# A new hand-written order of all steps in a gated-recurrence kernel followed by an MLP

## The chip, the core and the metric

The kernel runs on one core of a Trainium2 chip. The metric is device time in microseconds (us) of one launch. It is measured over several launches, and a separate launch is profiled; the profile is one execution and has its own time.

## What is computed

The first half is a gated linear recurrence with a complex decay, for 4 batches, 8 heads, 768 tokens and 48 features a head. Its output, 3072 tokens of 384 features, goes through an MLP with 2048 hidden features and a leaky activation with one slope a feature.

```python
scale = np.minimum(mag, 0.999) / (mag + 1e-06)          # mag = |a|
a_re_n, a_im_n = (a_re * scale, a_im * scale)
for t in range(S):
    new_re = ar * S_re - ai * S_im
    new_im = ar * S_im + ai * S_re
    S_re, S_im = (new_re + kv, new_im)                  # kv = outer(k_t, v_t)
    y[:, :, t] = einsum('bhd,bhde->bhe', q[:, :, t], S_re)

h = x @ w_in                                            # x: (3072, 384)
g = np.maximum(h, 0.0) + alpha * np.minimum(h, 0.0)
out = g @ w_out
```

All of it is float32; the MLP's weights arrive as float64 words and are turned into float32 on the core.

## The kernel before

The 768 tokens of a batch are cut into 6 chunks of 128; 4 batches give 24 **units**. The decays are prepared for whole chunks at a time by nine **gate tasks** (one chunk, then two, then seven times three). A gate task is a long alternation of DVE and ACT operations (lines 248 to 427, some small ones on POOL). It writes its decays to DRAM (line 321) and, at its end, its phases (the products of lines 422 and 425 on DVE, then the transfers of line 427).

A unit loads its queries and keys (KQ, lines 575 and 577), its phases (PP, line 586), its decays (T, line 593) and its values (V and VL, lines 602 to 628). It then runs:

- the rotation of KQ by PP, one DVE operation of 2.3 us (line 648);
- six levels of doubling block size. A level copies weights on ACT (W, line 719), makes 16 products of 32x32 on PE (line 662), multiplies KQ by decays on DVE (line 701) and masks the products into A (line 686 on DVE, 683 on ACT);
- 8 transposes on PE (line 736), copied to KT by ACT (line 738), and the outer products of keys and values (line 747), which DVE adds into the state St (lines 777 and 780);
- the unit's output in PSUM: 4 products that clear it (line 759), 48 products A x VL (line 768) and 16 **state products**, the earlier state times the queries (line 793);
- ACT's copy to yT (line 807) and two stores to DRAM (line 812).

The MLP runs over 14 groups of tokens: two of one unit, ten of two, two of one. A group loads x (xT, line 825), makes 16 hidden blocks of 3 products each (`features`, line 841; 256 tokens wide, 128 in the groups of one unit), applies the activation on ACT and DVE (lines 848 and 850), and adds 16 output products of 384 columns for each 128 tokens (`outputs`, line 860). Rows then leave through ACT (line 870) and line 873.

Everything that sets who comes first is **one string, ORDER**. Each task is a Python generator that stops at every step; a letter resumes the task of that letter. A to I are the gate tasks, J the loads of KQ, PP and T, K the transfers that spread the values' rows, L the loads of V and VL, M the raw weights, N and O their conversion, P to Z and a to m the 24 units, n the loads of x, and o the whole MLP. The instructions reach each engine's queue in the order in which the letters emit them, and an engine works its queue in that order. All DMAs are issued by SP, so a letter also fixes a transfer's place on SP's queue. Buffers (three of KQ, one of PP, two of T, one of V and VL, two of xT, two PSUM tiles for hidden blocks) bound how far a task can run ahead. The arguments of the `yield`s, such as `PE(0.47, ...)`, are costs for the planner that made ORDER; at run time `step` returns None and nothing is read from them.

```python
    def run(self, order):
        for c in order:
            next(self.tasks[self.LETTERS.index(c)], None)
```

```python
    with tc.manual_schedule():
        for i, g in enumerate(GATES):
            plan.add(gates(i, *g))
        ...
        plan.add(loads_x())
        plan.add(all_mlp())
        plan.run(ORDER)
```

Of the kernel before, what the change touches and what calls it, by code (L numbers as in the profile page):

```python
# [27 lines left out]


ORDER = (  # L30
    "AAAAAAAAAABBAMMABMAAAAAMNAAAMMAAAAAAAAABKAAAAAAJKBBNBAKJANAAAJONNAAAAAAOBNOAAAAAAAAAAAJAAAKKAAAAAAKK"
# [9 lines left out]
    "LLLLLLooooUTooULLooEooooULJETDTooDooooooDDTDUoooTTooooLooDUoDooKLTTDooooTToooooDDDTETToUUoooTooToTTT"
    "TTnoDoooooooooTLLLUUoooKooLLLLLUTUoLooLooFEJLTUUUULoooooEoJUEooooooUUUUUUEJooEULEEooooooooUoTKEEEToo"
    "EEUVoTToTUUoEoooVVoooooEooooooVUJVVoUFoVUUooTVoUVVUVEUUJJJJUEEEEEEEEEEEEUoUJJTLTVUVFVoVoFWooFVJVVooo"
    "VFooooUUUVVVJUWVKVVUVWWoooooVLLWLLLLLWLLEEEEEEEEEEEEEEEELVVoVLLoWWoLJVVoWoVUoVWVVVooEooooJEEUWWWoVVV"
    "VWVVVVoWWJJJJJJXooEFnFooEEoEELLLLLLLLKJEFLoooVEoooEEooLEooWLLLWXoWLooooWWEoooEooooKEXEWWWKoVVooooooo"
    "KXooEooooXWJWJXXoooWooooWWFoVVoWVXWooooooWWFXFWWWFEWWFFFFGFXooLJLLLLLLXWooooooWFWFXXJFoooFooooFWoFXX"
    "oLLFoGooooJJooooooJFoWFXXXFWFFFWFFFoFooWFoXFFWXooooooFooooooooooXXXXYooooooooGJFWWFXXFXYooFFoooXLLXX"
    "LFFooooooooooLoooYXGLoooXJoooooGYXXFXXFFXXXXXFFFFFFFJYYFJnYJXoGYoooooJFFFFFFFFFFFFFFFLFJJYZFoooooooL"
    "ooGoYZYXXXGJYYZooXooZZoGoooooYooYXoFooooYYYYYYYYYZZoooZFZFFFooooFXJYZoLLLoYoYJYoLLLLLLLKYoYoYooZGLLY"
    "YKYYYYJFYZYYJKXFFFGGooYYJYLLLJLFFLoooooaFFFoYLFFFoFoJJJooZLFZYYYGYYaGLoLLoLLooooooooFLLFoFFFoooooooo"  # L50
    "ooooZoooaZaJZaoooGoZaJZnGZZZZZaooooooooooooaaooaGaZZoooaooZoJoooJGoZZooZoZoooZaHZZZGGoGGGGGGGZZZZZGZ"
    "GaZKKHLGGGoooooaGGoooooooGooobooGoaoooaoaaaaaoooLoGGbooobbZaaaoaaZooaJZZZLJoLLLLLLLLLLoGGGGaaoooGboG"
    "GJoooZaJJoabboooooooaaaaaaaaGHJZHGJJbbbbGGGLGGooooooHoooobaobJJaGGGGGGGGaaaooJJboocooooooobbcoGGbcHb"
    "ooGbLJJKooooooooooooocbGbHcHcLGLcGGKooooooLLbHbLcbbaabGGGGGGooooobbKcGbGJGJGcLLGGGooooHGGcobbbcHoooo"
    "bbLooooLLLLbbbnbcGHbbbbbJGGGdoooooGoLLoocbGGGGGccbooooJJboooGKobGGoGHooLLLLLLoooGHbbbboLooooooooGcLL"
    "LdddccccHdooooocccooooooocdcccdooJoddoLoooooHJcdocLHdJoHdHKHdcoJJooooooocccccIIccoccceooJJooHLLLoooo"
    "oooLoLdeLcHHcccHHHHccccoLLLHHLHHHHnooHoHHHLooooooooHJooooeIdLLLooooooooddooooooeeeHHHHdooHoHHdHeeooo"
    "oooooodddddeooooooodJdoJoeooHHHHHHHHHHHoodoodododeoododooodeedddddddHHdHHHHHHIeeKKeeKHJJooJfooooIooo"
    "ooeeeKeddfoLLdeeooeoeoooJooLooooddLLHHHHHHHHHHHHHHJeedIeeeLfooLLoLLooefLLLLeIofdooeeeHHeeeeeeHHefIIf"
    "IfHfJHHJHJdJooooooeeJJJJJeeeoeegLJHLHHLLofoLLLLLLLofIoooooooooIHooLJffooJoHoooooHogofHoHHIoooooIoooo"  # L60
    "noffoHHooooogfoofoooooffIffffLgoogoooofgooLoffIfJoofoIfIIooJoIfoofooooffffffffffgKggooooohLLLooLhogo"
    "oIoLgghgoooooJJILLLoooLLLffILLfhIIIgghoooooooooohgooJJhgfJJfhhKffggIgggKgooohoooohhggggJghooohoogogo"
    "IgIgooooggIgggggggIhJhoLLgLgIIIIJgIogooooKKoIoooIhooLooILhIoooooooggKJIIIIIIIIJJoooooiLIhoooIIIIoIoo"
    "oooihnooIhhhhihhiooooIiooooLLLLLLiihhLLohohoooooohohohoooohhIIIIhhIhhhhhhJJJIooooooooooJJLiioihiioio"
    "JIoLooLiiijoooooIIIooooIIIioIIIIIIIIIIoiiiiiihhhhhjLLhjLoLLLLLLLiJIIIIIIIoooooojooooojoiijjjoooiooio"
    "jiiooooiLhIIIIIoIoioiiiiiiJLLLLLILooooooLLoooiIioooiiiiiIijjoIiiiIIooooooooooooonJooJJJJooojjjjooooo"
    "ooooooooooooJoLLjjoojojjoojoLkojLjjoooooooooojjkokoooooojjkkjookkoooojjjooLooooLjkjjjjJkkooojjkjjkoo"
    "oooJoooooooookJJokjjJJLllLooLokLkoLoLLLjjkkLkkkLLLLLkkjJjjkooooooooooooJkollkokkJoooooooooookllllooj"
    "kokooJJJlJokoooookkkkJkkkkkkkkkllLLlkLLooomkkkoooolooooooLollooooolloJooomloooonoooooooooooooooooooo"
    "oooooooooollllJlmmooooooooooolmmlooooooolllooolLLLLolomLLLLLllooooooooollloolmlmmmmoooooooomlllloooo"  # L70
# [882 lines left out]
```

## Time and profile before

| what | us |
|---|---|
| median of 3 runs | 863.18 |
| lowest and highest of them | 861.69, 864.44 |
| time of the profiled execution | 859.8 |
| span of its instructions | 858.1 |
| PE busy (matmuls) | 704.7 |
| DVE busy | 655.6 |
| ACT busy | 427.1 |
| POOL busy | 186.3 |
| hidden products (line 841), busy | 303.4 |
| output products (line 860), busy | 297.5 |
| decay products on KQ (line 701), busy | 178.3 |

The span runs from the first instruction to the last; the profiled execution's own time has 1.7 us more. Busy times of different engines overlap, so they don't add up to the span: an engine matters in the stretch where the others wait for it. PE busy counts matmuls as they overlap in its pipeline, and a busy PE may be slow, because its granted clock was below full in parts of the first 275 us. A matmul of two float32 operands appears as two records, as does its weight load; so counts on PE are twice the products in the code, except for the transposes and for line 759.

The first hidden product of the third group (the first group of two units) starts at 246.82 us; the last rows leave after the last output product, at the end of the span.

### The profile page before, as it was taken

Reading aid. Unit: us, or ns where it says so; the run is one execution under the profiler, and the core shown is the slowest. Engines: PE = TensorE matmul, PEld = TensorE weight load, DVE = VectorE, ACT = ScalarE, POOL = GpSimd, SP = SyncE. Lnnn points to the kernel's source line nnn. Section 1 sums busy time; section 2 is a strip of 40 time slices with the busy share of each in tenths; the row PEclk is TensorE's granted clock in tenths of the full one; section 3 lists DMA queues with packets and bytes.
Section 4 is the critical chain, followed back from the end, with each engine's and each line's share of the span. In section 5 each row is a group of like instructions: output and inputs, shape, how many; then the busy total and the mean of one; then the engine's idle time right before and its main releaser. Section 6 shows DMA issues by size and latency. Waiting matters only on the chain.

```text
span 858.1 us, 26855 instructions
## 1 busy us (share of the span) xinstructions
PE 704.7 (82%) x11488; PEld 529.1 (62%) x11488; DVE 655.6 (76%) x996; ACT 427.1 (50%) x913; POOL 186.3 (22%) x293
## 2 busy tenths in 40 slices
PE   0000414976898999999999999999999999999998
PEld 0000313655676777777777777777777777777776
DVE  5999999999976899789978987798867665444212
ACT  7757578576434565554555554654334234233221
POOL 5212323457313200440034005300052000000000
PEclk9999965896999999999999999999999999999999
DMA  7689977977688778669684787865674766221110
GB/s 222 170 211 232 269 175 178 241 154 154 170 194 165 159 195 207 125 135 227 160 182 110 180 216 147 158 170 127 176 155 74 173 121 134 63 51 38 39 39 9
DMA packets 194559, 130.92 MB, mean 153 GB/s; under 512 B 74504, under 2 KB 186248, under 8 KB 194440
## 3 DMA queue, kind: packets, MB, share of 16 engines
q1 hardware_dynamic: 194440, 129.20, 64.9%
q8 instruction: 90, 1.47, 0.8%
q14 instruction: 29, 0.24, 0.1%
HBM read 100.82 MB, written 35.71 MB: 159 GB/s over the span
## 4 chain that ended last, share of the span: by engine, by line
PE 74%; DVE 15%; SPq 3%; issue 3%; DMA 3%; ACT 2%; DVEq 0%; ACTq 0%
PE ps_o L860 29%; PE ps_h L841 29%; PE ps_lv L662 5%; PE ps_y L768 4%; DVE KQ L701 3%; PE ps_kv L747 3%; PE ps_y L793 3%; SPq L556 2%; DVE gate L336 2%; PE ps_kt L736 2%; DMA V<-in_v_dram 1%; DVE gate L338 1%; DVE gate L316 1%; DVE gate L296 1%; DVE gate L422 1%
## 5 line engine op out<-in xcount | busy, mean ns | idle before, releaser
L841 PE MATMUL ps_h<-xT,w_in_sb 128*128 128x256 f32 (+1 forms) x1344 | 303.4, 357 | 0.0
L860 PE MATMUL ps_o<-w_out_sb,g_sb 128*128 128x384 f32 x768 | 297.5, 501 | 7.2 <-DVE g_sb L850 7.1
L841 PEld LDWEIGHTS ps_h<-xT,w_in_sb 128*128 128x128 f32 x1344 | 233.8, 193 | 69.9 <-issue 1.7
L701 DVE TENSOR_TENSOR KQ<-KQ,T 96x1024 f32<-96x1024 f32 x144 | 178.3, 1248 | 44.1 <-PE ps_lv L662 41.1
L848 ACT ACTIVATE g_sb<-ps_h 128x256 f32<-128x256 f32 (+1 forms) x224 | 78.9, 353 | 235.8 <-PE ps_h L841 235.1
L850 DVE SCALAR_TENSOR_TENSOR g_sb<-g_sb,al,ps_h 128x256 f32<-128x256 f32 (+1 forms) x224 | 97.5, 437 | 126.8 <-ACT g_sb L848 126.4
L860 PEld LDWEIGHTS ps_o<-w_out_sb,g_sb 128*128 128x128 f32 x768 | 137.4, 192 | 58.0 <-DVE g_sb L850 9.7
L662 PE MATMUL ps_lv<-KQ,W 96*32 96x32 f32 x3840 | 56.5, 205 | 57.5 <-ACT W L719 54.1
L719 ACT COPY W<-KQ 96x512 f32<-96x512 f32 x120 | 74.3, 623 | 55.4 <-DVE KQ L701 54.1
L662 PEld LDWEIGHTS ps_lv<-KQ,W 96*32 96x32 f32 x3840 | 44.6, 116 | 83.0 <-ACT W L719 62.4
L662 PE MATMUL ps_lv<-KQ 96*32 96x32 f32 x768 | 12.0, 206 | 68.2 <-DVE KQ L648 52.6
L511 POOL TENSOR_SCALAR top<-top 128x768 f32<-128x768 f32 x16 | 43.5, 2721 | 84.3 <-ACT top L503 84.0
L648 DVE TENSOR_TENSOR KQ<-KQ,PP 96x2048 f32<-96x2048 f32 x24 | 55.0, 2292 | 0.0
L662 PEld LDWEIGHTS ps_lv<-KQ 96*32 96x32 f32 x768 | 9.5, 119 | 71.8 <-DVE KQ L648 52.6
L336 DVE TENSOR_TENSOR gate<-gate 128x576 f32<-128x576 f32 (+5 forms) x84 | 48.3, 575 | 3.1 <-ACT gate L308 1.3
L768 PE MATMUL ps_y<-A,VL 64*48 64x64 f32 x2304 | 42.2, 223 | 8.6 <-issue 6.8
L683 ACT ACTIVATE A<-ps_lv,rows 128x64 f32<-128x64 f32 x144 | 39.2, 331 | 19.4 <-PE ps_lv L662 19.0
L336 POOL TENSOR_TENSOR gate<-gate 128x72 f32<-128x72 f32 x42 | 19.0, 451 | 127.2 <-ACT gate L366 124.4
L768 PEld LDWEIGHTS ps_y<-A,VL 64*48 64x48 f32 x2304 | 39.6, 125 | 11.0 <-issue 8.9
L422 DVE TENSOR_TENSOR gate<-gate 128x1152 f32<-128x1152 f32 (+2 forms) x36 | 43.5, 1233 | 0.1
L807 ACT COPY yT<-ps_y 48x256 f32<-48x256 f32 x96 | 32.0, 366 | 21.1 <-PE ps_y L793 20.4
L686 DVE TENSOR_TENSOR A<-ps_lv,mask 128x256 f32<-128x256 f32 x96 | 39.5, 414 | 0.0
(100 smaller groups left out, 774.5 us busy)
## 6 DMA issues: line engine op xcount, KB each, us to landing
T<-decs SPq DMA_DIRECT2D x48, 384.0 KB
PP<-phs SPq DMA_DIRECT2D x48, 193.5 KB
KQ<-in_q_dram SPq DMA_DIRECT2D x48, 192.0 KB
decs<-gate SPq DMA_DIRECT2D x7, 1152.0 KB
...
```

The source lines that it names most:

```text
L336: on(4 * k).tensor_tensor(out=m, in0=w[:, 1::-1].unsqueeze(2).to_broadcast([P, 2, 2, k]), in1=pairs_of(u), op=ALU.mult)
L422: TT(out=m[:, a], in0=U5[:, 1 + a], in1=turned(off3, o)[:, a].unsqueeze(1).unsqueeze(3).to_broadcast([P, L // 2, nb, 2]), op=ALU.mult)
L511: nc.gpsimd.tensor_scalar(out=top, in0=top, scalar1=F64_SMALL, scalar2=None, op0=ALU.max)
L648: nc.vector.tensor_tensor(out=KQ, in0=KQ, in1=bass.AP(tensor=PP.tensor, offset=PP.offset, ap=[PP.ap[0], (1, 2), (P + 1, H), (1, P)]), op=A ...
L662: nc.tensor.matmul(t[64 * i + j:64 * i + j + HC // 2, p], lhsT=weights(4 * i + p)[:, j:j + HC // 2], rhs=q_[:, m * g:m * (g + 1)], start=T ...
L701: nc.vector.tensor_tensor(out=x, in0=x, in1=m, op=ALU.mult)
L719: nc.scalar.copy(W.rearrange("p n t -> p (n t)").rearrange("p (m h) -> p m h", h=h), halves(KQ[:, 1].rearrange("p n t -> p (n t)"), h)[:, ...
L768: nc.tensor.matmul(o, lhsT=Vp[h][64 * i:64 * i + 64, s, e_ * D:(e_ + 1) * D], rhs=a, start=False, stop=False)
L841: nc.tensor.matmul(p, lhsT=w_in_sb[:, f // 2, kk, f % 2 * P:(f % 2 + 1) * P], rhs=x_of[m][:, kk], start=(kk == 0), stop=(kk == NK - 1))
L848: nc.scalar.activation(gt, p, AF.Relu, scale=-1.0)
L850: nc.vector.scalar_tensor_tensor(out=gt, in0=gt, scalar=al_1[:, f:f + 1], in1=p, op0=ALU.mult, op1=ALU.add)
L860: nc.tensor.matmul(sums[0], lhsT=gt[:, c * P:(c + 1) * P], rhs=w_out_sb[:, f], start=(f == 0), stop=(f == NF - 1))
```

## The change

Only ORDER changes. The new string has the same 4316 letters, each as often as before, so the same instructions with the same operands are made. The first 10 letters and the last stretch of o's stay; between them nearly every stretch differs. Instructions of one task keep their order among themselves; what moves is how the tasks interleave on PE, DVE, ACT, POOL and SP.

```diff
 ORDER = (
-    "AAAAAAAAAABBAMMABMAAAAAMNAAAMMAAAAAAAAABKAAAAAAJKBBNBAKJANAAAJONNAAAAAAOBNOAAAAAAAAAAAJAAAKKAAAAAAKK"
-    "KBABKLMAMKKKAAAAAAAAAAAAABBAAAAAAAAAALLLNLNOBBBBBBBBBBBBBBBOKKLJBBJBCOCNBBBBNNBBBNNNKNBBNNBBBBBOPBBO"
-    "BBOOBBBBBBBLLBBBBBPCPPBBBBBBBBBBBOBJBBBBCBBBNBCBBJBPMMJBLBBBLBOPBLMLJJJPPBBCLBOBONOPBBMCCCCCPNPPCLCN"
...
-    "NQRoRQKoQQQRDKDJQEREoDONJDDDMDDDQooooDoDooooooRQooooooQooEDoooDoRRRRoooOooOOooooooDRRRJRoJDSooooooRD"
-    "RoRRLooQQooELoSOOOLLLLLLLDDDLLLRQQQSRRKKoLDEooSoQooOoDRooRooLoSoDoooEDDooRoooRRROSRRRREoooooQRREDDDD"
...
+    "AAAAAAAAAAAABBMJJBAAAAAAABJJBAAAMMAAAAAAAMNNMBBNLAAAAAAAAAAMNAAAAAAAAONAAAAAALLLLLLLAAAAAABOBAANAAABA"
+    "ABMLLAABBBBAAOAABBABANKKKLAKKKBKKKKKKKKMLNAKAONBOKAAAMANAABOBBBAABABAAABABAABBBBBBBOBKBBNOBBBBBBBNBB"
+    "BBBBJJNONBBBNOBNBOBOBBBJJBBPOPBBBBBBBBNCBPCPBOBBBBMKBBBBPOBOMJCPBOBBBJJOBBBNBCCKPNCCCCBBBJMLPPBNONNP"
...
+    "RCQNOnLCCLOMLCCQCCCLQLLLQOOKCOQoONNCNCooDJKKCCCRCooCoCLQDQQJDLQoQDDRDDRoQoDDoDooooooooDDNLDKRRRooQoo"
+    "QoQDDooQooooJQNJEREoooDKQoDQMDQDQDLDDDQoLLLLLLLLLoooooDDSDQEoRRODRDoooEoooooDREQQNooSDQRooooDoRDRRRD"
...
```

More of the change, by code (lines that the diff above doesn't have):

```diff
@@ L30 @@
 ORDER = (
-    "AAAAAAAAAABBAMMABMAAAAAMNAAAMMAAAAAAAAABKAAAAAAJKBBNBAKJANAAAJONNAAAAAAOBNOAAAAAAAAAAAJAAAKKAAAAAAKK"
-    "KBABKLMAMKKKAAAAAAAAAAAAABBAAAAAAAAAALLLNLNOBBBBBBBBBBBBBBBOKKLJBBJBCOCNBBBBNNBBBNNNKNBBNNBBBBBOPBBO"
-    "BBOOBBBBBBBLLBBBBBPCPPBBBBBBBBBBBOBJBBBBCBBBNBCBBJBPMMJBLBBBLBOPBLMLJJJPPBBCLBOBONOPBBMCCCCCPNPPCLCN"
-    "CCCNNCCOPPKJCPCCJMPPJJJJPCNCOCCCCCCCCPOOOOCCCONNNPPQQCOCMCMDPPPPPPPPPPPPPPPPPNPPCNCNCCCNCPONPOCCCQCN"
-    "NPKCQCCCPCPCJQQQPQQQCCCCOCCCCQCPNOJQQCOJDJPJJPPKQPDDONJDQCCCCCCCCCQCCOOCQCDQQOLOCCCCCCCDKMRnQQQMKQQK"
@@ L36 @@
-    "KKNCKOKOCCCCKMRJQoOCCQQQQNQoJCDQoCCOCLOCCNCCQONLoooLLLDLLDNNDLLDoooDDLoRoNLoRDoRNNDRDRooLLNRJRRDDDDD"
-    "NQRoRQKoQQQRDKDJQEREoDONJDDDMDDDQooooDoDooooooRQooooooQooEDoooDoRRRRoooOooOOooooooDRRRJRoJDSooooooRD"
-    "RoRRLooQQooELoSOOOLLLLLLLDDDLLLRQQQSRRKKoLDEooSoQooOoDRooRooLoSoDoooEDDooRoooRRROSRRRREoooooQRREDDDD"
-    "SDDDDDDoDEESJJSJEEQDJJRJJJSKSSSTSDDLLLRRRRRRLLLESSSDLLTSDEnToTDDSTSETTSSSSLSJTSSSLLDDDDDDDDEEDDDDooS"
-    "LLLoKTSooJSoEooSEoDDDDSEETSSSSSSJJSSSSETTTDJEEETDJooEEEEoUTJJJJLLoEooEEJTooDSoooooEoooTDDDTDoSSSSSoL"
@@ L41 @@
[L41 to L70, printed above, removed]
@@ L71 @@
-    "ooooooooooomlmlmlmoolommllllnoooooooooooooommLmmmoooooooooooooooooooooooooomoLomLooooomommoLLLLLoooL"
-    "LLmmmLLooooooooooooooooooooooooooooooooooooooooooommmmmmmmmoommmmmoooooomnoooooooooooooooooooooooooo"
+    "AAAAAAAAAAAABBMJJBAAAAAABJJBAAAMMAAAAAAAMNNMBBNLAAAAAAAAAAMNAAAAAAAAONAAAAAALLLLLLLAAAAAABOBAANAAABA"
+    "ABMLLAABBBBAAOAABBABANKKKLAKKKBKKKKKKKKMLNAKAONBOKAAAMANAABOBBBAABABAAABABAABBBBBBBOBKBBNOBBBBBBBNBB"
+    "BBBBJJNONBBBNOBNBOBOBBBJJBBPOPBBBBBBBBNCBPCPBOBBBBMKBBBBPOBOMJCPBOBBBJJOBBBNBCCKPNCCCCBBBJMLPPBNONNP"
@@ new lines @@
+    "CBBPCCOOCCNPOCCCPCPPPMCCCCLJJJDCPCPMPCNNNKCJPDNQCOCPCNCMCOPPPPCCQJPPPJJPJJJPPPPCCCCQCCQQQCDPPCCNOOCK"
+    "OPPNCCCQCNNONCPQCQPQPCCPCCCPCPMDLPCOCQCPOCCCPRJOPCNPCJCCCQQPPCCNCOCCLLPQMJCQCCDCQROQQCCCKJNLCCRCKRNR"
+    "RCQNOnLCCLOMLCCQCCCLQLLLQOOKCOQoONNCNCooDJKKCCCRCooCoCLQDQQJDLQoQDDRDDRoQoDDoDooooooooDDNLDKRRRooQoo"
+    "QoQDDooQooooJQNJEREoooDKQoDQMDQDQDLDDDQoLLLLLLLLLoooooDDSDQEoRRODRDoooEoooooDREQQNooSDQRooooDoRDRRRD"
+    "ooRRQQRoQQoooDooRDDDooRRRRRRDNNNDDOJLooJLDDDDDDSSQLoooDoLQoRRRRSRRORRESRRROSoooooSSoJJoNoooSSKSEDDJJ"
@@ new lines @@
+    "JJJJJDLoTEJSDDDSSEERDooODSSoEODRETDJTOTSEoDDTTSSSSSOSLTTLRoJnLooRKOTESSLLLLTSJooEToSLSLSDLLoooLooLDD"
+    "DDDDDDDDDDDSJEDDEKTKKEKSKoooDooooDDoSREoRESSSSSESToSLLSULDEooSTSoooooDoooDLLTTEoToooooEooEDTJTSELLLS"
+    "LLEELLSUESDDLJoLDTTSDDoooToooooDTSTooTooooooDoTooooJJooTTooUUoTToooooJTDJUooTUTTonEETTTTDEoDToDDoooo"
+    "ooUoooooLLooUEooooooooTUETEoooEoUTUooLLLLLLooEooooELLoLUJEFoooooooEEULooooTUEEEEEEEoUoooUooooUUUTToJ"
+    "UoLUooTVooVEEEUUUUUooVUooToooUoJVUEEJEEEEEJoJUoVVoVUUJoVoUUUUUUEVVUFVoTVJJEEEEEEEJJVVoooVVVVVWoooooF"
@@ new lines @@
+    "ooEJVLLEVVVKFTLLEVUEEEEEVoUWWoWEEEVooooWoEEUUVVUoVEVWWWFooooVVooooVLLLUFLVLLLLLooLJVWWoUUWoooEEEEooV"
+    "VJWWVVVEWJoVJJEVFJoLnVFEVVEWJoVVEELoEVVVEooooEWWooooooWoJoXooooooFoEEVoooJWELWooooooooWWoooWooEWooLo"
+    "WXJLWXXELLLLLLWooWooooLooFWooFFoooooooLLoWJFFFFFFFXoooGooWoJoXWWWWWWWWWWXGFFFFFFoooooJLJJJXFFooFXoWF"
+    "WXWFWFoFXXoooYooGooLLoooooooFFFooFWFXoGWJKWJFooooooFFoooXoXoFFooWFooFooXXXXXoLLLLXFFLFLoXLoLXXJoJooo"
+    "oYXLLFoXXXoooXoYYXGooGKKYXoXoooFoooooFFFFFFFLoXXXXXXXXXFGYFFXJFFJnFYKYYoooooFFFFFFFFFXXFFFXJXXJYJZoo"
@@ new lines @@
+    "XoooooJKoZYYYFYYYoZZooFoYFoooooFFFooYZXZYYFooYYooZZoooZoooYKYYYYYFJLZZLZLLLooooYYLLLLooLLLLLooYoooYF"
+    "YYYYJJYJYYYYZFoJGLGJaooooFFFFFFoooFFoYaYYZYYFZooooooooJYYYZZZFLKoZZZZooooLLFFoLLooooaZFoooooLnaaZFoo"
+    "ooooooooooGGooGLoaooZooGGGZooaoGGGoooZGoooZZoaaaoaoZooZZaooGaJoJLLFLLLLZZZZZZaJJooooooZZGGGZaZZaGJaH"
+    "abHGKoLJbZZaGaJoooaJooooZZaooZobooooGaooLLZLaLGooabaGGLbGGooaooooLLLabGGGLaHaLooooooooooooLGGLGGGGGK"
+    "KGGabaooooooooJGKGKoooGGGGGGGGbaaaaaaaGGGGHHHHboHooobJKJGJJboooooooooooaaoGJJbbHcoababooooooooGGGGGG"
@@ new lines @@
+    "oooGGGGGGGKJooaabcbcaooJooGooooobocbHbbbbHbbcoboooooobbcbGGGHboGocoocbooJJoboobGGJJLLLbHHGLLLLLLLLLL"
+    "LdoooobbbbbbbbbcbcaHcooGGcoKcHHoooGnoocbJccooGGoooJGLGLcGdbcLJGbbobbGocdGccdLbccoooodocooooooooLLLLG"
+    "cGGddddooooocooooGGoocoooLoccdddcoocoLodooHHcJLoooooooooLLLccccGJJHJcccHHHHdcccccHccIJIJHoHoooooooHH"
+    "HoHHcccHHHoHoJoooooooHHHoIdoeoooooLLooooooodHIHJKHoooooooodoIHHHJeenoLLHHeeHHHHHLHHoooooooHooHLLLLLd"
+    "ddddeedLdeeIoooooooooooHLLedodoodddoodJoooedeLooeHHHHdoooJoooIJoodddddddHddHHHHeHHHHHIHHHHeJfHLLdooo"
@@ new lines @@
+    "ooeoooLLLLLLLLLLoLoeeeeooeooooeoIIooooeJJefdddeoHHHeHooddoeeoIIffooHoooeeooooeoodJLdoJJfffeeeeeefeeH"
+    "IHJJJLLLLLLLoLLLoeIHeHHfgJHHHoooooLooooooooffLLKHoJooooHHfofoHoeeeeHeHLefeoHooooeoKfooooIfHooHoooooo"
+    "oofffgofggoooooooIooooffgoJfoogJffoofoonffofgfHooffoJJoooKKfIfIffgfffoKKKKJooJfooooooooofgfgfgoooooo"
+    "LogIghIoIIoJoooooohJghghhffffgghohooooogggghoggoooohogooooohhIIghggoIghooogoLLLLLLLLLLIJJfLLJoogggJJ"
+    "JoofggghgggIIIhIIIIhLLLoioooooooooghIIIIJhgIghhhhhhhJoooooogIIoooooooIggoggghhiooIohhhooIIIooooioIoo"
@@ new lines @@
+    "ohIhoooooIohhoIooIIIoIoooIooLoLoLoJoLLLLniiooooJioJLLIIiIILLhhhIIIIIhIhJoohhoiioooooohhhhhihhooiiIoI"
+    "ooooooIIIIhJIiIIIJooJJJLLiijJooIIoooooohhIIooiiooooooLLLIIiIIijjLLILLLiiiiiJLLooojooooooooooooooojjI"
+    "jjiiioIIIIojooLLoooooiiiooooIoiooiiiiiiiIIIIIIIIioooooooooooiooLLiiiiijojiiiioooooooInjJoooooooooooo"
+    "ooojjjjooooJJJJJooJojooookLLLLooooojoooojjjjooooooooooojjjkjkokooooojjjjooLoooLoLLLkjoojLLLjjjjjjjjj"
+    "koJJookJJkklooooooooookLLLLLLLLkokoooooLLkkkjkkljoojjokkkJJkooooooooljjklkooooollkklkoLLkkloooLoLjoo"
@@ L73 @@
+    "kooooookjlkJJJJookkkkkkkkkkkkkklloJJJkokkkolooollomoooooooollolooolmllJlllomloooooomlmmlnoLooooooooo"
+    "ooooooooooLmLLLmLoooooLoLLoLooooLLmllllLLooooooooooolloooooooooomllmllllmmmmoooomooomLmoooooolommmmm"
+    "mloooloooooLooooooollmmlolollllomoLLLmLooooooooooooooooooooooooooooLLooonoooLLLoooomooooooooooommmoo"
+    "ooooooooooooooooooooooooooooLooooooooLoooooooooooommmmmmmmmmmmmmmnoooooooooooooooooooooooooooooooooo"
     "oooooooooooooooooooooooooooooooooooooooooooooooooooooooooooooooooooooooooooooooooooooooooooooooooooo"
```

## The prediction

> **What bounds the kernel now.** First the page's slices: DVE is at nine tenths or more in slices 2 to 10 (21 to 215 us), PE from slice 12 to the end, and the granted clock dips in between.
>
> ```profile
> span 858.1 us, 26855 instructions
> PE   0000414976898999999999999999999999999998
> DVE  5999999999976899789978987798867665444212
> PEclk9999965896999999999999999999999999999999
> PE 74%; DVE 15%; SPq 3%; issue 3%; DMA 3%; ACT 2%; DVEq 0%; ACTq 0%
> ```
>
> The last line, the chain that ended last by engine, says the same. Then busy time by stage (us of PE, PEld, DVE, ACT, POOL, then clock, DMA share, GB/s), cut at the first hidden products of groups 1 (202 us), 2 (247) and 3 (303):
>
> ```profile
> 0.00:98.00 98.00, 4.36 (x224) 3.58 (x224) 85.16 (x185) 67.88 (x99) 31.31 (x42) 1.00 0.84 218
> 98.00:202.00 104.00, 58.46 (x1347) 45.07 (x1348) 101.69 (x158) 72.53 (x127) 41.12 (x34) 0.73 0.76 184
> 202.00:247.00 45.00, 39.17 (x761) 31.05 (x762) 38.90 (x57) 17.27 (x47) 15.22 (x21) 0.90 0.76 179
> 247.00:303.00 56.00, 51.84 (x986) 39.33 (x986) 45.21 (x61) 30.10 (x74) 15.49 (x34) 0.97 0.83 170
> 303.00:858.00 555.00, 550.91 (x8174) 410.11 (x8172) 384.69 (x539) 239.34 (x569) 83.11 (x163) 1.00 0.58 131
> ```
>
> Up to 202 us DVE is the bound (98% from 98 on), from 303 PE (99%). Between them DVE idles 6.1 + 10.8 us and PE also waits: this is the handover. So the time is DVE's work before the handover, the losses in it, and PE's work after it.
>
> Last, PE in order of time. A steady stretch gives prices, two stretches of the handover give waits:
>
> ```profile
> 540.43 0.59 PE L841 MATMUL ps_h<-xT,w_in_sb 128*128 128x256 f32 x2
> 540.96 0.46 PE L662 MATMUL ps_lv<-KQ,W 96*32 96x32 f32 x32
> 541.35 1.13 PE L841 MATMUL ps_h<-xT,w_in_sb 128*128 128x256 f32 x4
> 542.31 1.45 PE L860 MATMUL ps_o<-w_out_sb,g_sb 128*128 128x384 f32 x4
> ...
> 208.23 0.95 PE L768 MATMUL ps_y<-A,VL 64*48 64x64 f32 x53
> 211.66 0.87 PE L768 MATMUL ps_y<-A,VL 64*48 64x64 f32 x43 [2.48 <-issue]
> ...
> 268.67 1.86 PE L768 MATMUL ps_y<-A,VL 64*48 64x64 f32 x56 [2.74 <-issue]
> ...
> q8 instruction: 90, 1.47, 0.8%
> ```
>
> One hidden product (two records) costs 0.53 us before the visit to small tiles (540.43 to 540.96), two cost 0.96 after it; undisturbed it is 0.432. The waits of 2.5 and 2.7 us lie inside a run of products A x VL and are put to "issue": no semaphore ended them.
>
> **What the Trainium skill says.** "TensorEngine Tiling (Array Packing)", section Tiling Modes: changing the tiling mode drains the array. The trace agrees: over all steady visits the last MLP product before one costs 0.093 us more, the first after it 0.104 more, and the last small product 0.133 to 0.156 in place of 0.02 to 0.06: 0.31 us a visit. The transposes (full width) cost only 0.029. "Runtime: NRT & Kernel Launch", section Instruction fetch mechanics: instructions come in pages of 256, the next one fetched while one runs. The trace agrees: 90 fetches of 16 KB on q8, and numbering PE's instructions, its "issue" waits in line 768 come at numbers 1731, 3523, 5314 and 6339, all 194 or 195 beyond a multiple of 256. The same section calls this mostly hidden; here it is not where a page holds only small products. A page that waited took 4.92, 5.06 and 4.98 us from its start to the next one's (at 206.75, 286.33, 599.78), while pages of 4.46 and 4.71 us later passed without a wait. So a page costs about 5 us at least, 4.5 when DMA is light. "TensorE: Matmul & The Clock Gate", Part 1: an idle window of about 3.4 us halves the clock. After the wait at 268.67 the clock record is half for 3.4 us, which costs half of that, 1.7.
>
> **The change, part by part.** No instruction is added or removed, so I price positions. I gave DVE's instructions their durations of the trace (a pipelined one counted to the next one's start, 655.7 us in all) and PE's products their steady start-to-start distances with the visit prices above, and summed both along the order of each program.
>
> 1. *DVE's work ahead of the handover.* Ahead of the first hidden product of group 2 stand 227.4 us in the old order and 225.1 in the new: -2.3. Ahead of group 1 it is 188.2 and 188.4, so the gain lies between them. ACT's work there is 155.1 and 154.5, POOL's 88.4 and 88.4.
>
> 2. *PE's work behind it.* The sum over all products is 675.0 and 676.2. From that product to the end it is 597.0 and 597.4: +0.4. Behind it visits to small tiles go from 82 to 83 (0.31); a differing mix inside visits is the rest. For the old order the trace has 607.8 (246.82 to 854.6); the 10.8 above the sum are waits and slow clock, 8.0 of them before 303 us.
>
> 3. *Page waits in the handover, behind group 2's start.* Before: 2.95 + 0.55 + 0.98 = 4.5 us at pages 20, 21 and 24, counting from 0 (each from the end of PE's last weight load). In the new order pages 20, 21 and 24 hold 4.5, 3.4 and 3.98 us of work; at 5 us a page that is 0.5 + 1.6 + 1.0 = 3.1. Net -1.4. Bounds: DMA can delay a fetch (the one of 260.78 started 5.2 us later), which makes it +2; if data waits cover the pages, -4.5.
>
> 4. *Page waits from group 3 on.* Old: two, 0.68 and 0.26 at pages 64 and 76, which hold 3.95 and 5.55 us of work. New: the shortest hold 4.3, 4.36 and 4.4. At 4.5 us a page the shortfalls fall by 0.4, at 5.0 they rise from 2.5 to 4.2. I take +0.3; ends -0.4 and +1.7.
>
> 5. *The half-rate windows* behind waits (238.1 to 241.5, 268.8 to 272.3) I cost at nothing: they follow PE's idling, about as much as before. Ends -1.7 and +1.7.
>
> 6. *Transfers past SP's queue*, at nothing. Walking SP's queue with 0.55 us an issue and each producer at its place in DVE's and PE's work, the least lead of a transfer on its use is, old and new: KQ 6.9 and 4.4, PP 5.6 and 3.3, T 4.6 and 5.8, V 10.2 and 10.7, VL 4.2 and 4.6, x 5.3 and 5.8 us (estimates). They hide under work already queued on PE or DVE. The trace shows one late VL (1.83 us at 236.63), so a lead near 4 can cost about 2. The shortest, PP 3.3 for unit 16, falls after 500 us where DVE idles a quarter of the time: that idle time hides it.
>
> 7. *Round trips PE to DVE and back* (line 701, W, line 662, line 701). DVE work between two neighbours of a unit falls short of 2.5 us by 4.3 us in all ahead of group 2 in the old order and by 2.2 in the new; between groups 2 and 3 by 6.9 and 9.0. I take them as even; ends -2 and +2.
>
> Sum: -2.3 + 0.4 - 1.4 + 0.3 = -3.0 us. Against the profiled execution, 859.8 - 3.0 = 856.8 (span 858.1 to 855.1). That execution lies 3.4 below the median, 863.18, so a median of **860.2 us**. A measurement of this kernel tells a change from none at about 0.3%, 2.6 us; the forecast lies just beyond.
>
> **Rivals.** *The wait only moves.* For: pages 20, 21 and 24 are short in both orders, and items 1 and 7 partly cancel between groups 2 and 3. Against: DVE's work ahead of group 2 is a plain count. Then 863 to 864.
>
> *More gain.* For: from group 1 to group 3 pages fall short of 5 us by 11.7 us in all in the old order and 5.1 in the new. If that whole difference shows and a half-rate window goes with it: -2.3 + 0.4 - 6.6 + 1.7 - 1.7 = -8.5 (with item 4 at its end), 854.7. Against: ahead of 247 us PE's waits are mostly covered by DVE.
>
> *Slower: late phases stall DVE.* Place: the rotations of units 0, 1 and 3, the first to use a gate task's phases. DVE's work between the task's last operation and that rotation shrinks from 16.1, 20.2 and 29.5 us to 12.6, 12.1 and 15.9. In it a store of phases must land, then a load of PP. Before, for unit 0, the operation ended at 33.6, the loads were issued at 38.7 and 39.4, and the rotation at 50.22 did not wait. If the load takes as long as the store, it is in by about 44.5, 11 us after the operation (estimate); that fits into 12 barely. DVE works its queue in order: behind a waiting rotation stand the gate work and levels of other units, and PE waits for these. Each us beyond 12 costs about one for each of the two first units. At 16 us it is 3.4 + 3.9 + 0.1 = 7.4, so 867.6; from 13.5 on the gain of 3.0 is gone. For: DMA is busiest in these 100 us (share 0.84). Against: the store went quickly there.
>
> **How the numbers follow.** Forecast 0.38 (own range 857.5 to 862.5; 0.27 faster, 0.11 within 0.3%). More gain 0.12, all faster. The wait moves 0.18 (0.15 within, 0.03 slower). Late phases 0.32 (0.30 slower, 0.02 within). So faster 0.39, within 0.28, slower 0.33. The range, 853.5 to 868.5, leaves out the lower part of the second case and the upper part of the last.
>
> **What would show it.** Item 1: the first hidden product of group 2 near 244.5 us in place of 246.8. Item 2: from group 3 to the last product 552 us as before, within 2. Items 3 and 4: "issue" waits at 194 or 195 beyond multiples of 256, about 3 us between 247 and 303. Late phases: idle DVE time ahead of line 648, none before. The forecast is wrong if DVE idles over 5 us more before 247 us, or if PE waits in the steady stage.

## The result and the profile after

The new order takes 859.47 us (median of 20 runs, 856.23 to 864.19), the old one beside it 862.38 (20 runs, 858.61 to 865.27). The ratio is 0.9969, 95% interval 0.9955 to 0.9982: 2.7 us less, where 3.0 were forecast. The profiled execution has a span of 855.8 us, where the old one has 858.1. First its page: the span, the slices of PE, DVE and the clock, and the chain that ended last by engine.

```profile
span 855.8 us, 26849 instructions
PE   0000425757997999999999999999999999999998
DVE  5999999998996898789879987788946657633112
PEclk9999956987999999999999999999999999999999
PE 72%; DVE 14%; DMA 4%; issue 3%; SPq 3%; ACT 2%; POOL 1%; DVEq 0%; ACTq 0%; POOLq 0%
```

The picture is that of before: DVE bounds the first 200 us, PE the rest, with a handover between. Busy time by stage, cut at the same times as before (us of PE, PEld, DVE, ACT, POOL, then clock, DMA share, GB/s):

```profile
0.00:98.00 98.00, 5.92 (x231) 4.74 (x232) 85.58 (x186) 67.23 (x100) 36.01 (x42) 1.00 0.90 227
98.00:202.00 104.00, 59.42 (x1389) 47.30 (x1389) 101.74 (x159) 72.17 (x126) 39.57 (x38) 0.77 0.83 189
202.00:247.00 45.00, 40.88 (x773) 32.99 (x772) 40.87 (x66) 19.76 (x53) 15.44 (x18) 0.96 0.71 179
247.00:303.00 56.00, 48.75 (x918) 37.28 (x917) 43.09 (x55) 29.75 (x74) 19.09 (x34) 0.97 0.81 160
303.00:856.00 553.00, 546.34 (x8185) 406.30 (x8183) 380.52 (x534) 237.49 (x561) 84.40 (x163) 1.00 0.58 130
```

The clock of 1.00 in the first row, here and before, is not measured: the record of the granted clock begins at 107.3 us in this trace and at 105.0 in that of before, and what stands ahead of its first entry is counted as full.

From 202 to 247 us DVE idles 4.1 us in place of 6.1, and the clock is 0.96 in place of 0.90. From 247 to 303 it is the other way: PE is busy 48.75 us in place of 51.84, DVE 43.09 in place of 45.21. So the change wins in the one stage and loses in the next. The places in time of each group's first hidden product (line 841) and of the end of the last output product say how much, in us:

| | before | after | difference |
|---|---|---|---|
| group 1 | 202.6 | 200.2 | -2.4 |
| group 2 | 246.8 | 239.6 | -7.2 |
| group 3 | 302.7 | 297.5 | -5.2 |
| group 4 | 356.0 | 352.4 | -3.6 |
| group 8 | 577.4 | 576.1 | -1.3 |
| last output product | 854.6 | 852.2 | -2.4 |

The sum came out as forecast, the terms did not: at group 2 the new order is 7.2 us ahead, not 2.3, and it then gives back almost 5. What it gives back shows in PE's weight loads of the new kernel, in order of time, where the idle time before one is put to "issue":

```profile
261.10 1.72 PEld L768 LDWEIGHTS ps_y<-A,VL 64*48 64x48 f32 x59 [2.10 <-issue]
...
269.03 0.14 PEld L662 LDWEIGHTS ps_lv<-KQ,W 96*32 96x32 f32 x2 [3.01 <-issue]
...
287.17 0.51 PEld L768 LDWEIGHTS ps_y<-A,VL 64*48 64x48 f32 x29 [0.56 <-issue]
...
294.56 0.21 PEld L662 LDWEIGHTS ps_lv<-KQ,W 96*32 96x32 f32 x13 [1.05 <-issue]
...
322.47 0.61 PEld L793 LDWEIGHTS ps_y<-KQ,St 96*48 96x48 f32 x18 [0.80 <-issue]
...
497.63 0.40 PEld L841 LDWEIGHTS ps_h<-xT,w_in_sb 128*128 128x128 f32 x2 [1.90 <-issue]
```

All six are at instructions 194 or 195 beyond a multiple of 256 in PE's stream: they are page waits. Between groups 2 and 3 they sum to 6.7 us, 4.3 before by the same column; behind group 3 to 2.7, where before has one of 0.6 (at 604.76). Of the rival "late phases" nothing is there: all 24 rotations (line 648) together waited 0.5 us.

### The profile page after: what moved, and what is told of

It is laid out like the page before. It is cut to its first block, busy times and chain, and to the rows that moved or that the text cites. A ratio compares the mean times of both kernels' runs of the same rounds, so it can differ in the third digit from the quotient of the medians.

```text
span 855.8 us, 26849 instructions
## 1 busy us (share of the span) xinstructions
PE 701.3 (82%) x11488; PEld 528.6 (62%) x11488; DVE 651.8 (76%) x996; ACT 426.4 (50%) x913; POOL 194.5 (23%) x293
## 4 chain that ended last, share of the span: by engine, by line
PE 72%; DVE 14%; DMA 4%; issue 3%; SPq 3%; ACT 2%; POOL 1%; DVEq 0%; ACTq 0%; POOLq 0%
PE ps_o L860 28%; PE ps_h L841 28%; PE ps_lv L662 5%; PE ps_y L768 4%; PE ps_kv L747 3%; PE ps_y L793 3%; DVE KQ L701 2%; DVE gate L336 2%; PE ps_kt L736 2%; DVE gate L338 1%; DVE KQ L648 1%; DVE gate L422 1%; DMA VL<-in_v_dram 1%; DMA g_sb<-in_w_out_dram 1%; DMA T<-decs 1%
## 5 line engine op out<-in xcount | busy, mean ns | idle before, releaser
L860 PE MATMUL ps_o<-w_out_sb,g_sb 128*128 128x384 f32 x768 | 294.1, 497 | 1.5 <-DVE g_sb L850 1.4
L701 DVE TENSOR_TENSOR KQ<-KQ,T 96x1024 f32<-96x1024 f32 x144 | 176.4, 1234 | 46.2 <-PE ps_lv L662 42.1
L511 POOL TENSOR_SCALAR top<-top 128x768 f32<-128x768 f32 x16 | 44.2, 2763 | 63.8 <-ACT top L503 63.8
L336 POOL TENSOR_TENSOR gate<-gate 128x72 f32<-128x72 f32 x42 | 21.8, 519 | 100.6 <-ACT gate L366 97.8
```

Source lines behind the costliest of these rows:

```text
L336: on(4 * k).tensor_tensor(out=m, in0=w[:, 1::-1].unsqueeze(2).to_broadcast([P, 2, 2, k]), in1=pairs_of(u), op=ALU.mult)
L511: nc.gpsimd.tensor_scalar(out=top, in0=top, scalar1=F64_SMALL, scalar2=None, op0=ALU.max)
L701: nc.vector.tensor_tensor(out=x, in0=x, in1=m, op=ALU.mult)
L860: nc.tensor.matmul(sums[0], lhsT=gt[:, c * P:(c + 1) * P], rhs=w_out_sb[:, f], start=(f == 0), stop=(f == NF - 1))
```

## The experiments

Eleven kernels were run, each with the old order beside it. Most are new strings ORDER: a letter only resumes a task, so the first part of one string can be joined to the letters of the other that are not yet used. "Until group 2" means up to the step that emits the first hidden product of group 2. In such a diff only the row with the seam is shown; the rows behind it all differ from the one string and agree with the other from a few dozen letters on.

### Where the gain is: three cuts

The first theory (A) put the gain ahead of group 2 and a loss behind it. The new order until group 2, then the old one (against the new order):

```diff
-    "ooUoooooLLooUEooooooooTUETEoooEoUTUooLLLLLLooEooooELLoLUJEFoooooooEEULooooTUEEEEEEEoUoooUooooUUUTToJ"
+    "ooUoooooLLooUEooooooooTUETEoooEoUTUooLLLLLLooEooULLFJLUUUULEJUEooooooUUUUUUEJooEULEEooooooooUoEEEToo"
...
```

> Order: the new one until the first hidden product of group 2, then the remaining steps in the old order. In the two traces the new order starts group 2 at 239.58 us (old 246.82, so 7.24 earlier) and needs 612.6 us from there to the last output product (old 607.8). Theory A, the gain lies wholly ahead of group 2 and the new order loses 4.8 us behind it by its own order: 7.2 us faster than before, ratio 0.992. Theory B, what is lost behind group 2 is the price of starting it early (its data and DVE's work aren't there yet), whatever the order: about 3 us faster, ratio 0.9965, with the group 2 start at 239.6 and the loss between 240 and 303 us. By pages of 256 PE instructions this order has, from group 3 on, 0.0 to 0.9 us short of 4.5 to 5.0 us a page (old 0.8 to 2.5, new 0.4 to 4.2).

The reverse, the old order until group 2 and then the new one (against the old order):

```diff
-    "TTnoDoooooooooTLLLUUoooKooLLLLLUTUoLooLooFEJLTUUUULoooooEoJUEooooooUUUUUUEJooEULEEooooooooUoTKEEEToo"
+    "TTnoDoooooooooTLLLUUoooKooLLLLLUTUoLooLooFEJLTUUUULoooooEoKToooEoooooooEEooooTEEEEEEEooooooooUUUTToJ"
...
```

> Order: the old one until the first hidden product of group 2, then the remaining steps in the new order. Theory A: group 2 starts at 246.8 as before and the rest costs 4.8 us more than before, ratio 1.0055. Theory B: the rest costs what the old rest costs, 607.8, ratio 1.000. Pages: six PE instructions fewer stand ahead, which moves every page border; from group 3 on the pages fall short of 4.5 to 5.0 us by 3.9 to 9.7 us in all, so theory A with pages gives 3 to 6 us more than the new rest, ratio 1.006 to 1.012, with its waits at 194 or 195 beyond multiples of 256.

And the new order until group 3:

```diff
-    "VJWWVVVEWJoVJJEVFJoLnVFEVVEWJoVVEELoEVVVEooooEWWooooooWoJoXooooooFoEEVoooJWELWooooooooWWoooWooEWooLo"
+    "VJWWVVVEWJoVJJEVFJoLnVFEVVEWJoVVEELoEVVVEooooEWWooooooWoJoXooooooLLLLLLKJFLLLLLXWLWWEoKEXEWWWKoooooo"
...
```

> Order: the new one until the first hidden product of group 3, then the old one. The new order starts group 3 at 297.50 us, 5.15 earlier than the old. Theory A: 5.2 us faster than before or a little more, ratio 0.994, since the old rest costs 552 us and its pages here fall short by 0.0 to 0.1 us only (old 0.8 to 2.5). Theory B: as new_until_g2, ratio 0.9965.

Measured against the old order: new until group 2, 0.9939 (0.9916 to 0.9961, 854.88 us); old until group 2, 1.0055 (1.0038 to 1.0071, 866.02 us); new until group 3, 0.9954 (0.9942 to 0.9966, 856.84 us). Of theory A's ratios (0.992, 1.0055, 0.994) the first two lie inside these intervals and the third just below its own; of theory B's (0.9965, 1.000, 0.9965) only the third does, so A fits better, though not well. So the part ahead of group 2 is worth about 5 us, and the part behind it costs about as much alone. Multiplied, these two leave 0.9994, where the whole new order has 0.9969; their intervals together just allow that, so the halves need not simply add. How the first of them stands to the new order was not measured directly, and the two intervals against the old one (to 0.9961, from 0.9955) just touch.

### Which stage ahead of group 2

Two mechanisms were open: a late load of VL for the fifth unit, or the letters of a stretch as a whole. In the old order, PE in order of time has this wait:

```profile
236.63 1.33 PE L768 MATMUL ps_y<-A,VL 64*48 64x64 f32 x80 [1.83 <-DMA VL<-vsc]
```

Then the clock is half from 238.1 to 241.5 us, and DVE, also of the old order, stands still behind PE's slow hidden products and ACT:

```profile
240.98 0.35 DVE L850 SCALAR_TENSOR_TENSOR g_sb<-g_sb,al,ps_h 128x128 f32<-128x128 f32 x1 [3.65 <-ACT g_sb L848]
242.81 0.35 DVE L850 SCALAR_TENSOR_TENSOR g_sb<-g_sb,al,ps_h 128x128 f32<-128x128 f32 x1 [1.02 <-ACT g_sb L848]
```

SP issued that load at 231.42 us, behind a key load, two phase transfers and a store of value rows; in the new order it goes out at 218.97 and nothing waits. The theory (A1) was that this chain is the gain. It was tried from both ends. The old order with two letters L moved up:

```diff
-    "LLLLLLooooUTooULLooEooooULJETDTooDooooooDDTDUoooTTooooLooDUoDooKLTTDooooTToooooDDDTETToUUoooTooToTTT"
+    "LLLLLLooooUTooULLooEooooULLLJETDTooDooooooDDTDUoooTTooooooDUoDooKTTDooooTToooooDDDTETToUUoooTooToTTT"
```

> The old order with two letters moved: the last two VL loads of the fifth unit (lines 625 and 628) are issued right behind the eight before them, ahead of two phase transfers (line 417), one KQ load and one store of value rows, so about 2.2 us earlier (near 229.2 in place of 231.4 us). PE's order stays. Theory A1 (the late VL starts the chain: PE idles 1.8 us, drops to half rate for 3.4 us, DVE then waits for PE's products): the wait at 236.6 and the half-rate window at 238 go, group 2 starts 2 to 6 us earlier (241 to 245), and 1.5 to 4 us of it reach the end: ratio to before 0.995 to 0.998. Rival (the wait only moves to another load or to DVE): group 2 at 246 to 247 and ratio 0.999 to 1.001.

The new order with one L moved back:

```diff
-    "LLEELLSUESDDLJoLDTTSDDoooToooooDTSTooTooooooDoTooooJJooTTooUUoTToooooJTDJUooTUTTonEETTTTDEoDToDDoooo"
+    "LLEELLSUESDDLJoDTTSDDoooToooooDTSTooTooooooDoTooooJJooTTooUUoTToooooJTDJUooTUTLTonEETTTTDEoDToDDoooo"
```

> The new order with one letter moved: the VL load of the fifth unit from the spread rows (line 628) is issued near 225.5 in place of 219.0 us, just ahead of its first use in the program. PE's order stays. Theory A1: PE waits about 2 us for it near 229 to 231, a half-rate window of 3.4 us follows and DVE waits behind it: group 2 starts 2 to 5 us later than in the new order (242 to 245 in place of 239.6) and the end comes 1 to 3 us later, so the ratio to before is 0.998 to 1.001 where the new order has 0.997. Rival (the new order gains elsewhere, this load has slack): group 2 within 1 us of 239.6, ratio 0.996 to 0.998.

The load moved up went out at 227.86 us on SP of old_vl4_early and the wait was gone; group 2 started at 243.7 in place of 246.8, as expected. But the ratio is 1.0000 (0.9987 to 1.0013): the theory's 1.5 to 4 us at the end failed, nothing of the 3.1 us arrived there. Its profile shows 2.0 us of them given back by group 3 (a page wait of 3.31 us at 266.57 and twice the half-rate time, 3.5 in place of 1.7) and the rest and 2 us more at 605.18 us, behind a page wait of 1.86 and 3.4 us at half the clock.

In new_vl4_late, PE in order of time has the old order's wait again:

```profile
230.65 1.34 PE L768 MATMUL ps_y<-A,VL 64*48 64x64 f32 x80 [1.68 <-DMA VL<-vsc]
```

The stage from group 1 to group 2 of that kernel (us of PE, PEld, DVE, ACT, POOL, then clock):

```profile
202.10:240.40 38.30, 33.82 (x709) 27.25 (x708) 36.30 (x54) 16.72 (x46) 16.48 (x15) 1.00 0.66 168
```

The wait costs nothing: the clock stays at 1.00, DVE idles 2.0 us of 38.3, the ratio is 0.9973 (0.9959 to 0.9987), that of the new order. So A1 falls as an account of the gain at the end. A PE wait for the same load is followed by half the clock and a long DVE wait in one order (1.8 us) and by neither in the other (1.7 us). That DVE had work queued there, or that the clock did not fall, are two possible reasons; no run tells them apart.

The rival was the stretch as a whole. The new order until group 1, then the old one:

```diff
-    "JJJJJDLoTEJSDDDSSEERDooODSSoEODRETDJTOTSEoDDTTSSSSSOSLTTLRoJnLooRKOTESSLLLLTSJooEToSLSLSDLLoooLooLDD"
+    "JJJJJDLoTEJSDDDSSEERDooODSSoEODRETDJTOTSEoDDTTSSSSSOSLTTLRoJnLooRKOTESSLLLLTSJooEToSLSLSDLLoooKRRDDD"
...
```

> The new order up to the first hidden product of group 1 (near 200 us), all later letters in the order of the old string. If the gain is made between groups 1 and 2 (theory A1: the late VL and what follows it), this kernel keeps only the 2.4 us that group 1 is early by in the profile, or nothing: ratio 0.997 to 1.001, and the wait for VL near 235 us is there. If it is made ahead of group 1 (rival: DVE's backlog is the bound and the later order doesn't matter), the ratio is 0.992 to 0.995 as with the cut at group 2.

And only the middle: old until group 1, new until group 2, old again:

```diff
-    "LLLoKTSooJSoEooSEoDDDDSEETSSSSSSJJSSSSETTTDJEEETDJooEEEEoUTJJJJLLoEooEEJTooDSoooooEoooTDDDTDoSSSSSoL"
+    "LLLoJJJTTJTSooDDSJDDTKKEKSKoooDooooDDoSEoESSSSSESToSLLSULDEooSTSoooooDoooDLLTTEoToooooEooEDTJTSELLLS"
...
```

> The old order up to the first hidden product of group 1, then the letters that the new order has up to its first hidden product of group 2 and that are not yet used, then the rest as in the old string. The runs so far put the gain of the new order between these two points (T from group 1 to group 2: 44.2 us before, 37.9 to 39.4 with the new letters up to group 2). Theory B (these letters alone make it): group 1 at 202 to 203, group 2 at 240 to 242, end 3 to 5 us earlier, ratio 0.994 to 0.9965. Rival C (the new letters ahead of group 1 are needed too, because PE's work of that stretch is pulled in front of group 1 there: 46.5 against 44.9 us): group 2 at 244 to 247, ratio 0.997 to 1.000.

Until group 1: 0.9980 (0.9972 to 0.9989), a small gain of its own; the wait for VL that was expected there near 235 us is down to 0.4 us (at 236.75). Only the middle: 0.9939 (0.9915 to 0.9963), as much as the whole new order until group 2. Theory B of this last run holds for the place: some 40 us of the string, from group 1 to group 2, make the larger part of the gain. The anatomy of that stage in the old order:

```profile
202.60:246.80 44.20, 38.37 (x758) 30.27 (x757) 38.09 (x57) 17.10 (x46) 14.62 (x21) 0.91 0.76 180
```

New order:

```profile
200.20:239.60 39.40, 35.11 (x710) 28.63 (x709) 35.51 (x54) 16.80 (x45) 16.96 (x18) 0.96 0.70 174
```

New until group 2 (new_until_g2):

```profile
202.80:240.70 37.90, 34.02 (x710) 27.34 (x709) 36.52 (x55) 16.72 (x45) 16.65 (x15) 1.00 0.70 171
```

Only the middle (new_middle_only):

```profile
203.00:242.20 39.20, 36.05 (x742) 29.13 (x741) 35.43 (x54) 16.01 (x45) 16.83 (x18) 0.95 0.83 196
```

And the new order with its page borders moved, a run that is described below (pages_shift_32), with PE's wait at a border in it:

```profile
205.40:247.80 42.40, 36.90 (x709) 29.82 (x708) 35.94 (x55) 16.68 (x45) 15.78 (x15) 0.91 0.68 170
...
237.47 0.80 PE L841 MATMUL ps_h<-xT,w_in_sb 128*128 128x128 f32 x2 [3.46 <-issue]
```

Length is DVE's busy time plus its idle time. With the same cut for all kernels:

| letters from group 1 to 2 | kernels | length | DVE busy | DVE idle |
|---|---|---|---|---|
| old | before, old_until_g2, old_until_g3 | 42.6 to 45.9 | 37.7 to 38.1 | 4.9 to 8.0 |
| old, PE waits under 0.5 us for VL | old_vl4_early, new_until_g1 | 41.1, 40.4 | 37.8, 37.2 | 3.3, 3.2 |
| new | after, new_vl4_late, new_until_g2, new_until_g3, new_middle_only, new_until_g2_4_on | 37.6 to 39.4 | 35.4 to 36.5 | 1.1 to 3.9 |
| new, page borders moved | pages_shift_32, pages_shift_127 | 42.4, 46.6 | 35.9, 35.9 | 6.5, 10.7 |

So 1.2 to 2.7 us is DVE work that no longer lies there, wherever the borders are. The rest is DVE waiting, mostly for hidden products that reach it through ACT, and that goes with PE's waits and not with the letters alone. With the old letters DVE idles 8.0, 6.1, 4.9, 3.2 and 3.3 us where PE waits 3.4, 1.8, 0.6, 0.4 us and not at all for VL (old_until_g2, before, old_until_g3, new_until_g1, old_vl4_early). With the new letters it idles 6.5 and 10.7 us where a moved page border makes PE wait 3.5 and 4.2 us (237.47 above, and 234.26 in pages_shift_127). So a good part of the shorter stage is that neither of these waits falls badly in it; how much of that is owed to the letters and how much to where the borders happen to lie was not told apart.

What carries the gain from group 2 to the end is not fully shown either. The 3.1 us of old_vl4_early were lost, the 4.6 us of new_middle_only were not (0.9939); in their profiles the page waits over 0.4 us behind group 2 sum to 7.0 and 3.7 us, in before to 4.8.

The start of group 1, 2.4 us earlier in the profile of after, is not part of it: in new_until_g2, new_until_g3 and new_vl4_late, with the same letters up to there, it lies at 202.1 to 202.8, behind a DVE wait of about 3 us for POOL (line 511, near 195 us) that the profile of after does not have.

### What the new order loses behind

The new order's part from group 3 alone, behind the old one:

```diff
-    "VWVVVVoWWJJJJJJXooEFnFooEEoEELLLLLLLLKJEFLoooVEoooEEooLEooWLLLWXoWLooooWWEoooEooooKEXEWWWKoVVooooooo"
+    "VWVVVVoWWJJJJJJXooEFnFooEEoEELLLLLLLLKJEFLoooVEoooEEooLEooWLLLWXoWLooooWWEoooEoooVVVVoEVoooEoooooooo"
...
```

> The old order up to the first hidden product of group 3, then the new one. In the new order the rest from group 3 took 554.7 us in place of 552.0, and issue waits at page borders (294.6, 322.5, 497.6 us) sum to 3.7 us. Theory (the new rest costs by its pages): here the borders lie 5 instructions further in, and pages 39, 46, 54, 80 and 84 get shorter, so the shortfall to 4.7 us from group 3 on grows to 5.0 us from 1.4 of before; ratio 1.002 to 1.006, with issue waits of 4 to 7 us from 303 us on. Rival (the loss in the new order's rest was chance of one profile): 0.999 to 1.001.

The ratio is 1.0048 (1.0030 to 1.0066), 4.1 us, inside what the theory expected; so the loss is no chance of one profile. Its profile is one of its faster executions (862.61 us, the median is 865.73) and has two page waits beyond 1 us behind group 3, on PE:

```profile
412.10 0.99 PE L768 MATMUL ps_y<-A,VL 64*48 64x64 f32 x52 [0.99 <-issue]
...
502.92 1.56 PE L860 MATMUL ps_o<-w_out_sb,g_sb 128*128 128x384 f32 x4 [1.35 <-issue]
```

By its weight loads they are 1.14 and 1.75 us, less than the 4 to 7 expected in all. Only the first is at a page that was named as short (page 39). The second is the page that also waits in the new order at 497.63; the four others named passed without a wait of 0.6 us. So no fixed time for a page's fetch fits.

The traces hold the fetches themselves, packets of 16 KB on queue q8, and say more. From 203 us on, PE's weight loads paused for over 0.4 us at 85 page borders of the 13 kernels, and each time they went on 1.2 to 1.8 us after the end of the packet that belongs to the page border before. These packets took 0.9 to 1.6 us each. What varies is when a packet starts: 0.3 to 6.1 us behind the border before it at these 85 (5.2 us ahead of the wait of 269.03 in after), but 3.7 us ahead of that border at page 84 of old_until_g3, which lasted only 3.9 us and passed. So these waits end with the fetch; what holds a packet back was not tested.

Page borders themselves were moved in two kernels. The new order behind 32 extra products, which let every border fall 127 instructions earlier in the program:

```diff
+        pad = ps.tile([P, DM], F32, tag="o", name="ps_pad")
+        for _ in range(32):
+            nc.tensor.matmul(pad[:, 0:P], lhsT=ident, rhs=ident, start=True, stop=True)
         plan.run(ORDER)
```

> The new order with 32 float32 matmuls of 128x128 of the identity ahead of all steps, into a PSUM buffer that nobody reads; they run before 50 us, where PE has nothing to do. They put 127 PE instructions ahead of the rest and so move each border of a page of 256 instructions half a page, and nothing else. Theory pages (PE waits where a page holds less work than its successor's fetch takes, 4.5 to 5.0 us): from group 3 on 16 pages that hold 2 us of small products each fall wholly inside a page, 40 to 48 us short in all against 0.4 to 4.2 before, so 30 to 45 us slower than the new kernel, 890 to 905 us, ratio to before 1.03 to 1.05, with each wait 194 or 195 beyond a multiple of 256. Rival (the waits called issue come from transfers or semaphores): within 3 us of the new kernel, ratio 0.997.

And with 8 of them:

```diff
+        for _ in range(8):
```

> The new order behind 8 extra products of the identity with itself (32 instructions, about 1 us of PE time long before PE is the bound), so every page border lies 32 instructions earlier in the program. Page theory: at 4.7 us a page the shortfalls behind group 3 grow from 1.3 to 9.6 us, so the end comes 8 us later (5 to 10), ratio to before 1.003 to 1.009, and the issue waits behind 303 us lie at borders and sum to 6 to 12 us. Rival (a page costs only where it is much shorter, as with the shift by 127): 0 to 2 us later, ratio 0.997 to 0.999.

127 instructions: 1.0471 (1.0434 to 1.0507), 901.75 us, with 46.3 us of "issue" waits at 22 page borders. Two of them on PE:

```profile
331.77 1.32 PE L768 MATMUL ps_y<-A,VL 64*48 64x64 f32 x40 [4.76 <-issue]
...
521.64 0.38 PE L662 MATMUL ps_lv<-KQ,W 96*32 96x32 f32 x20 [4.13 <-issue]
```

The page theory's 890 to 905 holds. 32 instructions: 1.0174 (1.0152 to 1.0195), 874.45 us, twice the loss that was expected. From group 3 to the end it is as forecast, 562.8 us where the new order has 554.7 (+8.1), with waits at borders of 8.1 us (2.7 in the new order). The other 8 us are ahead of group 2, which starts at 247.8. It looks as if the extra products had a price of their own there. The first stage of pages_shift_32:

```profile
0.00:98.00 98.00, 9.87 (x248) 8.19 (x248) 86.01 (x187) 67.28 (x100) 36.50 (x42) 0.54 0.87 225
```

Without them the row says 1.00. But that is the clock that has no record yet; here the record begins at 4.7 us, with the extra products. PE's own times show no difference. First the new order, without and with a clock record, then pages_shift_32:

```profile
66.56 0.66 PE L662 MATMUL ps_lv<-KQ,W 96*32 96x32 f32 x32 [9.49 <-ACT W L719]
...
117.31 0.66 PE L662 MATMUL ps_lv<-KQ,W 96*32 96x32 f32 x32 [5.30 <-ACT W L719]
...
66.01 0.66 PE L662 MATMUL ps_lv<-KQ,W 96*32 96x32 f32 x32 [9.50 <-ACT W L719]
```

At 117.31 the record says half; at full rate 32 such products take 0.46 us (540.96, shown in the prediction). So PE ran at half rate in both kernels. And with four times as many extra products, in pages_shift_127, group 1 starts at 199.1 us, not later than in the new order (200.2). The extra products are therefore not the cause. Ahead of group 1 (205.4) the trace has the DVE wait for POOL named above and one of 1.4 us at 169.26 behind a page wait; from group 1 to 2 it has PE's 3.46 us at the border of 237.47, where the same page had cost the new order 0.5, and 6.8 us at half the clock from 236.8 on. That these are the whole 8 us was not shown.

Last, a small shift in new_until_g2, behind 280 us: two products that add zero to the seventh unit's output.

```diff
+                    for _ in range(2 if u == 6 else 0):
+                        nc.tensor.matmul(Y[64:64 + D, 1].rearrange("p s t -> p (s t)"),
+                                         lhsT=nothing[64:128], rhs=ident.bitcast(BF16)[64:128],
+                                         start=False, stop=False)
                 Vp = L["Vp"]
```

> The new order up to group 2 and the old one behind it, as in new_until_g2, and two more products in the seventh unit (near 280 us) that add zero to its output, 4 PE instructions in all. Behind them each page border lies 4 instructions earlier. Page theory: page 64, which had 4.46 us of work and a wait of 1.54 us at 600.4 us, then has 4.87 us; shortfall to 5 us from group 3 on falls from 0.4 to 0.1. The wait at 600 goes or falls below 0.7 us; with the half-rate stretch behind it, the end comes 0.5 to 2.5 us earlier than in new_until_g2: ratio to before 0.991 to 0.9935 (there 0.9939). Rival (the fetch time varies by more than the 0.4 us moved): 0.9935 to 0.995 and a wait at 600 as before.

PE in new_until_g2 had, at that page:

```profile
600.44 0.33 PE L662 MATMUL ps_lv<-KQ,W 96*32 96x32 f32 x15 [1.44 <-issue]
```

and in new_until_g2_4_on:

```profile
600.71 0.34 PE L662 MATMUL ps_lv<-KQ,W 96*32 96x32 f32 x17 [1.59 <-issue]
```

The wait did not shrink, and the ratio is 0.9942 (0.9920 to 0.9963). The rival holds: the packet of this fetch started 3.9 us behind its border in the first kernel and 4.5 in the second, so it varied by more than the 0.4 us of work that was moved. The ratio makes this the third kernel with the new letters from group 1 to 2 and the old ones behind that comes out at 0.994.

## Why the prediction came out right, and which of its terms did not

The forecast of -3.0 us met -2.7 (ratio 0.9969) by luck: the gain ahead of group 2 was put far too small, one term of the loss behind it had the wrong sign and another was far too small, and these errors cancelled.

- *Item 1 (DVE's work ahead of group 2, -2.3).* The work is right: in the stage from group 1 to group 2 DVE's busy time fell from 38.1 to 35.5 us, -2.6. What it "would show", group 2 near 244.5, is wrong: 239.6 here, 240.2 to 240.7 with the same letters, or one of them moved, in four other kernels.
- *Items 5 and 6 (half-rate windows and SP's queue, at nothing).* This is the step that failed, and it is the cost, not the counting: waits that DVE must sit out were priced at zero. DVE's idle time in that stage fell from 6.1 to 3.9 us, to 1.4 in the kernels with new letters until groups 2 and 3. Half-rate time cost PE about 4.0 us in the old order (an estimate: clock 0.91 over 44.2 us), 1.6 in the new one, nothing in those two. Item 6 saw the late VL but weighed it as a lead of 4.2 against 4.6 us, alike in both orders; in fact the load went out at 231.42 and 218.97, 3 us and 10 us ahead of the first product on VL (234.4 and 228.6). Moving that load alone brought group 2 forward by 3.1 us in its profile, and yet was worth nothing at the end (1.0000), so mending item 6 would not have been enough. Which of the other waits of the stretch makes the difference stays open.
- *Item 2 (PE's work behind, +0.4; 552 us from group 3 on).* That stretch took 554.7, beyond the margin of 2. PE was busy 0.6 us longer there (551.8 against 551.3), as its prices say too (549.7 against 549.1); the other 2.1 us are PE's idle time (2.8 against 0.7), which fits the page waits. One profile is a weak witness, though: with the old letters there, the stretch took 552.0 to 554.9 us in seven kernels.
- *Items 3 and 4 (page waits, -1.4 and +0.3).* They came out as +2.4 and +2.1. The fixed 5 us a page was the fault. The page that ended in the wait of 269.03 lasted 7.9 us, and the one from 287.17 to 294.56 lasted 7.4 and is not on the list of short pages; in old_until_g3 pages of 3.9 to 4.1 us passed. The packets show why: a fetch starts at very different times. Runs show the loss behind group 3 as such (1.0048); that its whole size is page waits was not shown. Between groups 2 and 3 the loss may be no property of the new letters: that stage took 55.8 us before, but 56.6 to 57.9 in the six other kernels with the old letters there, and 56.6 to 57.9 with the new (the shift by 127 apart).
- *Item 7 (round trips)* was taken as even. It was not tried by itself; the DVE idle time that went between groups 1 and 2 may in part be these.
- *The rivals.* "The wait only moves" is half of what happened: the gain at group 2 is real, and a large part of it is given back behind. "More gain", -8.5, was nearly there at group 2 and not at the end. Late phases did not show. (The prediction has its gain gone from 13.5 us on; by its own numbers that point is 13.85.)

The Trainium skill's page "Runtime: NRT & Kernel Launch", section Instruction fetch mechanics, calls the fetch mostly hidden. In this kernel the shift of all borders by 127 instructions cost some 5% (1.0471 of the old order's time in place of 0.9969), with 46.3 us of waits at borders, so here it is hidden only where borders happen to lie well.
